# Another order for the hand-written list of steps of slots 0 to 6 in an RWKV-7 and squared-ReLU kernel

## The chip, the cores and the metric

The kernel runs on one core of a Trainium2 chip. The metric is the device time of one execution in microseconds (us): the median of three runs for the kernel before, and a profiled execution beside it.

## What is computed

Two blocks follow each other. The first is a linear recurrence with a state of 40 x 40 for each of 4 batches and 8 heads, over 768 steps:

```python
for t in range(S):
    y[:, :, t] = np.einsum('bhd,bhde->bhe', rt, state)
    Sa = np.einsum('bhde,bhe->bhd', state, at)
    state = state * wt[:, :, None, :] - np.einsum('bhd,bhe->bhde', Sa, bt) + np.einsum('bhd,bhe->bhde', vt, kt)
```

The second takes y as 3072 tokens of 320 numbers: `h = max(x @ w_in, 0)`, then `out = (h * h) @ w_out`, with a hidden width of 2048. The weights come in 64-bit floats, which the kernel turns into 32-bit floats itself.

## The kernel before

The 768 steps are cut into 6 chunks of 128, and a slot is one chunk of one batch with all its 8 heads: 24 slots, numbered with the batches inside the chunk, so that slots 0 to 3 are the first chunk of the four batches and start from an empty state. In a slot the recurrence becomes matrix products. What remains serial in it is the inverse of a triangular matrix for each head, which is made in small blocks by POOL (GpSimd), for one or more slots at a time; such a group is a unit. Unit 0 is slot 0, unit 1 slot 1, unit 2 slots 2 and 3, unit 3 slots 4 and 5, unit 4 slots 6 and 7, and so on.

A slot passes through these steps. Each has a short word in the list that this change is about; the digit behind the word is the slot (for S, K the unit; for W, pa, pd a piece of the weights; for f a width).

- LW, LA, lk, lb, lr, lv: fetches of w, of b and a, and of k, b, r, v, each 160 KB from device memory into a ring of tiles. A fetch waits until the tile's last reader is done.
- e1.1 to e1.6, "early" (line 361): PE turns w, DVE (VectorE) makes running products of it (lines 372 to 381), PE turns b and a, DVE scales them (387, 388), PE multiplies them, and ACT (ScalarE) copies the product N out of PSUM (398 to 402). N is a single buffer.
- sE, sN: N's blocks are stored to device memory for POOL (kept_q, line 420), and the decays (kept_e, line 390). D loads decays back into one of two tiles.
- K (take, line 440): POOL's load of a unit's N blocks. S (solving, line 458): POOL's row-by-row solve; S3.99 runs it to its end and issues the store of the answer (kept_t, line 482).
- B (line 508): the load of the answer, A: of N. J, four times (lines 515 to 534): the inverse put together, DVE and ACT first, then two small sets of products on PE with ACT copies between.
- k, a, kb, rv, mrv: products of k, r, v with the decays, masked by DVE (line 347).
- x, then c seven times: the chain of the slot. Its fourth c is a set of transposes, its sixth the masked product RX, and its last gives the tokens (line 692) and the new state. ds and ts scale and turn the state where there is one.
- mv: eight DMAs that gather two slots' tokens for the second block. th and wh make the hidden layer for a quarter of it, sq squares it on DVE, q does a part of the second product.
- W: fetch of a piece of the weights. pa and pd: the ACT and the DVE instructions of one step that turns a piece into 32-bit floats (lines 275 to 292). pa copies one piece and finishes the one before; pd needs pa's result, and the next pa needs pd's.
- f: fill-in matmuls (line 264), identity times identity, whose result nobody reads. f10 makes ten blocks of 128 columns in matmuls of at most four blocks.

The slots from 7 on run through a function with a fixed order. Slots 0 to 6, with the early steps of up to slot 13, are issued by one list of 484 words, in which each word issues its instructions at once:

```python
        word, _, queue = word.partition("@")
        on_queue[0] = {"": nc.sync, "a": nc.scalar, "g": nc.gpsimd}[queue]
```

Each engine takes its instructions in the list's order, and each DMA is issued by the SP (SyncE) queue, or by ACT's or POOL's where the word ends in @a or @g. Nothing else schedules: a semaphore wait holds everything behind it on its engine. Weights have to be ready in 27 steps (pd26) before the first q. Two PSUM pools matter: ps_w with four banks, in which a transposed or multiplied tile stays until DVE or ACT has read it, and ps_f with two for the second block and the fill-ins.

Of the kernel before, what the change touches and what calls it, by code (L numbers as in the profile page):

```python
# [17 lines left out]
def kernel(  # L18
# [82 lines left out]
    def tick():  # L101
        for entry in line:
            entry[0] -= 1
        while line and line[0][0] <= 0:
            line.pop(0)[1]()
# [766 lines left out]
    def advance(u, n_):  # L872
        if u not in solves:
            solves[u] = [-1, solving(u, range(100))]
        while solves[u][0] < n_ and next(solves[u][1], "end") != "end":
            solves[u][0] += 1
        if n_ > 90:
            run(solves[u][1])
# [46 lines left out]
    }  # L925

    for word in """
e0.1 lv0 e0.2 e0.3 e0.4 e0.5 e0.6 sN0 K0 e1.1 e1.2 e1.3 e1.4 e1.5 f3 LW2 LA2 e1.6 sN1 LW3 S0.12 K1 k0 a0 rv0 mrv0 e2.1 kb0 f6 e2.2 lk1 LA3 LW4 lv1 e2.3 e2.4 e3.1 x0 e3.2 e2.5 sE2 f10 e2.6 sN2 e3.3 e3.4 e3.5 f8 sE3 f6 e3.6 LA4 f44 lv2 lr1 LW5 S0.99 B0 J0 S1.8 S1.20 sN3 K2 W0@g S1.99 J0 J0 f6 W1 rv1 lr2 f2 mrv1 c0 e4.1 e4.2 e4.3 k1 W2@g LA5 B1 c0 c0 kb1 e4.4 e4.5 sE4 c0 c0 c0 pa0 c0 D2 LW6 lb2 a1 e4.6 lk2 pd0 pa1 f10 pd1 J1 x1 f4 pa2 pd2 W3 sN4 A2 pa3 pd3 rv2 f4 e5.1 e5.2 J1 f24 lv3 J1 f3 c1 LA6 mrv2 f6 c1 lr3 e5.3 S2.4 S2.99 c1 f6 e5.4 c1 e5.5 sE5 B2 k2 f6 c1 kb2 a2 c1 c1 mv0 pa4 pd4 W4 pa5 pd5 e5.6 sN5 J2 K3 lk3 A3 lb3 D3 S3.99 LA7 e6.1 e6.2 f30 f10 x2 e6.3 e6.4 e6.5 f4 J2 rv3 J2 c2 c2 f4 c2 pa6 pd6 e6.6 f14 c2 mrv3 k3 pa7 B3 LW7 J3 c2 c2 kb3 lr4 sE6 J3 lv4 e7.1 pd7 c2 a3 f1 f4 pa8 J3 lk4@a e7.2 W5 x3 lv5 lb4 A4 D4 sN6 f8 rv4 W8 B4 W6 W7 c3 c3 e7.3 pd8 pa9 pd9 pa10 ds4 mrv4 e7.4 LA8 LW8 e7.5 c3 J4 k4 sE7 pd10 W11 f4 f8 c3 e7.6 W10 lr5 J4 sN7 c3 K4 pa11 pd11 kb4 J4 pa12 pd12 c3 W12 ts4 pa13 W9 f4 a4 pd13 W13 c3 pa14 D5 B5 mv1 pd14 e8.1 e8.2 LA9 f4 x4 W14 lb5 A5 lk5 pa15 pd15 pa16 f2 pd16 ds5 c4 rv5 f12 pa17 pd17 pa18 pd18 W15@a f2 th0 J5 pa19 pd19 W16 mrv5 c4 wh0 pa20 pd20 pa21 lr6 th0 c4 pd21 e8.3 lv6 LW9 wh0 W17 pa22 c4 e8.4 e8.5 LA10 k5 c4 kb5 c4 e8.6 pd22 W18@a sN8 th0 sE8@a wh0 J5 ts5 LW10 a5 th0 wh0 sq0 c4 D6 W19 sq0 e9.1 pa23 A6 lk6 S4.99 J5 e9.2 e9.3 x5 lb6 B6 e9.4 c5 f2 e9.5 sE9@a pd23 W20 e9.6 sN9 LW11 K5 rv6 lv7 LA11 pa24 ds6 e10.1 LW12 c5 e10.2 pd24 pa25 pd25 mrv6 e10.3 k6 J6 pa26 pd26 c5 th0 wh0 e10.4 LA12 e10.5 sE10@g lr7 c5 c5 th0 J6 kb6 c5 e10.6 sN10 e11.1 LW13 c5 a6 ts6 lk7 e11.2 sq0 mv2 wh0 x6 J6 D7 e11.3 e11.4 q0 e11.5 sq0 e11.6 sN11@g S5.99 K6 S6.99 q0 e12.1 q0 q0 e12.2 e12.3 c6 sE11 rv7 lb7 A7 c6 B7 q0 mrv7 q0 wh0 q0 e12.4 q0 ds7 J7 e12.5 c6 k7 kb7 th0 sq0 J7 a7 c6 sE12 e12.6 lr8 c6 LW14 ts7 wh0 c6 th0 th0 LA13 wh0 sN12 e13.1 e13.2 LA14 c6 q0 e13.3 e13.4 e13.5 x7 J7 A8 lv8 B8 e13.6 q0 lb8 sN13 D8 lk8 sq0 sE13 K7 S7.99
""".split():
        word, _, queue = word.partition("@")  # L930
        on_queue[0] = {"": nc.sync, "a": nc.scalar, "g": nc.gpsimd}[queue]
        kind = word.rstrip("0123456789.")
        at = word[len(kind):]
        if kind == "S":
            advance(*(int(n_) for n_ in at.split(".")))
        else:
            kinds[kind](int(at.split(".")[0]))
        on_queue[0] = nc.sync
        tick()
# [85 lines left out]
    for i in range(LAID, len(order)):  # L1025
        tc.no_sync_barrier()
        g = ready.pop(i)
# [41 lines left out]
```

## Time and profile before

| what | value |
|---|---|
| runs | 952.27, 954.84, 956.72 us; median 954.84 |
| profiled execution | 959.58 us, of which 957.7 us are the span from the first to the last instruction |
| PE (TensorE) busy | 913.9 us, 95% of the span |
| DVE, ACT, POOL busy | 451.0, 287.4, 531.9 us |
| mean granted PE clock | 0.959 of full speed |
| PE busy, list's part (0 to 337.7 us) | 299.4 us, of it fill-ins 73.6 us |
| DMA packets | 253222, of them 234143 under 512 bytes |

An fp32 matmul shows as two rows on PE and a transpose as one. A row's duration depends on the granted clock. A wait is put down to the semaphore that came last, so an engine that had long been done is not its cause.

### The profile page before, as it was taken

How to read it: one execution, taken by the hardware profiler on the slowest of the kernel's cores; microseconds unless marked ns; L12 is line 12 of the kernel's file. 1: busy time of each engine (PE TensorE's matmuls, PEld its weight loads, DVE VectorE, ACT ScalarE, POOL GpSimd, SP SyncE). 2: the span in 40 equal slices, each digit the busy share in tenths (PEclk: the TensorE clock that was granted, in tenths of full speed). 3: DMA queues.
4: the chain of work that ended last, by engine and by line, in shares of the span. 5: the costliest groups of instructions: out<-in, count | busy, mean ns of one | idle time of the engine just before them, and what ended most of it. 6: DMA issues, size and time to landing. Idle time of an engine off the chain costs nothing.

```text
span 957.7 us, 22644 instructions
## 1 busy us (share of the span) xinstructions
PE 913.9 (95%) x9156; PEld 725.4 (76%) x9156; DVE 451.0 (47%) x1064; ACT 287.4 (30%) x735; POOL 531.9 (56%) x1001
## 2 busy tenths in 40 slices
PE   5989989798999999999999999999999999999998
PEld 4646656567787887878888888888888887887776
DVE  4517556797873454543655553643334332231111
ACT  3123234545432333332433332222212222222111
POOL 4788507347007686429999849999858860000000
PEclk8888788889899999999999999999999999999999
DMA  9689757767784677895564786505474254120000
GB/s 110 116 158 186 145 117 140 162 167 152 151 134 115 130 153 133 165 178 109 113 96 91 122 177 116 110 21 84 105 138 76 38 108 76 40 36 9 13 14 14
DMA packets 253222, 103.36 MB, mean 108 GB/s; under 512 B 234143, under 2 KB 240159, under 8 KB 251967
## 3 DMA queue, kind: packets, MB, share of 16 engines
q1 hardware_dynamic: 246869, 83.43, 48.5%
q0 software_dynamic: 3600, 16.25, 6.8%
q10 hardware_dynamic: 2650, 2.25, 0.9%
q8 instruction: 72, 1.18, 0.5%
q14 instruction: 31, 0.25, 0.1%
HBM read 69.00 MB, written 30.92 MB: 104 GB/s over the span
## 4 chain that ended last, share of the span: by engine, by line
PE 72%; DMA 4%; DVE 2%; ACT 2%; SPq 1%; issue 0%; ACTq 0%; DVEq 0%
PE ps_f L87 40%; PE ps_w L87 13%; PE ps_c L87 12%; PE ps_w L331 4%; DMA dec<-kept_e 2%; DMA spares<-kept_m 2%; PE ps_c L593 1%; PE ps_c L666 1%; PE ps_w L577 1%; DMA hid<-in_moe_w_out_dram 1%; ACT N L401 0%; SPq L508 0%; DMA kept_t<-half_t 0%; SPq L146 0%; SPq L110 0%
## 5 line engine op out<-in xcount | busy, mean ns | idle before, releaser
L477 POOL TENSOR_TENSOR half_p<-half_n,half_t 128x126 f32<-128x126 f32 (+44 forms) x437 | 232.6, 532 | 75.7 <-DMA half_n<-kept_q 19.8
L479 POOL TENSOR_TENSOR half_t<-half_t,half_p 128x126 f32<-128x126 f32 (+44 forms) x437 | 249.1, 570 | 34.3
L87 PE MATMUL ps_f<-w_out,hid 128*128 128x320 f32 x768 | 218.7, 436 | 0.0
L87 PEld LDWEIGHTS ps_f<-w_out,hid 128*128 128x128 f32 x768 | 142.0, 190 | 54.0 <-issue 0.2
L87 PE MATMUL ps_f<-tokens,w_in 128*128 128x256 f32 x672 | 159.2, 391 | 0.0
L87 PEld LDWEIGHTS ps_f<-tokens,w_in 128*128 128x128 f32 x672 | 127.6, 195 | 19.5 <-issue 2.0
L764 DVE TENSOR_TENSOR hid<-hid 128x512 f32<-128x512 f32 x96 | 81.1, 883 | 50.1 <-ACT hid L757 49.7
L757 ACT ACTIVATE hid<-ps_f 128x512 f32<-128x512 f32 x84 | 50.0, 597 | 83.5 <-PE ps_f L87 83.5
L264 PE MATMUL ps_f<-ident 128*128 128x512 f32 (+2 forms) x148 | 73.6, 637 | 0.0
L347 DVE TENSOR_TENSOR RV<-ps_w,upper 128x512 f32<-128x512 f32 x48 | 30.9, 686 | 51.1 <-PE ps_w L87 50.8
L451 POOL DMA_DIRECT2D half_n<-kept_q x18 | 9.5, 530 | 80.1 <-DMA kept_q<-N 53.5
L692 DVE TENSOR_TENSOR tokens<-ps_c,dec 128x512 f32<-128x512 f32 x24 | 16.6, 690 | 76.6 <-PE ps_c L87 76.6
L372 DVE TENSOR_TENSOR_SCAN decay<-ps_w,ones 128x64 f32<-128x64 f32 x88 | 23.8, 271 | 59.7 <-PE ps_w L331 59.6
L264 PEld LDWEIGHTS ps_f<-ident 128*128 128x128 f32 x148 | 30.4, 223 | 27.5 <-issue 26.6
L347 DVE TENSOR_TENSOR RX<-ps_w,upper 128x512 f32<-128x512 f32 x48 | 30.9, 686 | 41.4 <-PE ps_w L87 41.0
L87 PE MATMUL ps_f<-tokens,w_third 64*128 64x256 f32 x336 | 46.9, 392 | 3.1 <-ACT hid L757 3.1
L543 DVE TENSOR_TENSOR kvT<-ps_w,dec 128x512 f32<-128x512 f32 x24 | 16.5, 688 | 63.1 <-ACT minus_x L653 36.0
L87 PEld LDWEIGHTS ps_c<-xr,T 64*64 64x64 f32 x768 | 28.5, 141 | 19.6 <-issue 16.5
L398 ACT COPY N<-ps_w 128x256 f32<-128x256 f32 x48 | 17.7, 368 | 83.8 <-PE ps_w L87 47.4
L555 ACT COPY rT<-ps_w 128x512 f32<-128x512 f32 x24 | 14.0, 585 | 77.7 <-PE ps_w L331 77.6
L87 PEld LDWEIGHTS ps_f<-tokens,w_third 64*128 64x128 f32 x336 | 31.0, 192 | 6.5 <-ACT hid L757 3.7
L87 PE MATMUL ps_c<-xr,T 64*64 64x40 f32 x768 | 34.5, 235 | 1.4 <-ACT xr L660 0.8
(146 smaller groups left out, 1407.3 us busy)
## 6 DMA issues: line engine op xcount, KB each, us to landing
dec<-kept_e SPq DMA_DIRECT2D x22, 633.8 KB
kept_e<-decay SPq DMA_DIRECT2D x19, 633.8 KB
in_w<-in_w_dram SPq DMA_DIRECT2D x24, 160.0 KB
in_b<-in_b_dram SPq DMA_DIRECT2D x24, 160.0 KB
in_ab<-in_a_dram SPq DMA_DIRECT2D x24, 160.0 KB
in_r<-in_r_dram SPq DMA_DIRECT2D x24, 160.0 KB
in_v<-in_v_dram SPq DMA_DIRECT2D x24, 160.0 KB
out_dram<-o SPq DMA_DIRECT2D x24, 160.0 KB
```

Source lines behind the costliest of these rows:

```text
L87: nc.tensor.matmul(o, l_, r_, start=start, stop=True, skip_group_check=True)
L264: nc.tensor.matmul(fill_bank[:, :n * 128], ident, ident.unsqueeze(1).to_broadcast([128, n, 128]), start=True, stop=True, skip_group_check= ...
L331: nc.tensor.transpose(p_[:, q * 128:(q + 1) * 128], pair(x_, q), ident)
L347: nc.vector.tensor_tensor(t_, p_, over4(upper), Alu.mult)
L372: nc.vector.tensor_tensor_scan(up[:, q, MID + 1:C + 1], wT[:, q, MID:], ones, 1.0, Alu.mult, Alu.mult)
L398: nc.scalar.copy(plain, p_[:, ::2].rearrange("s h (f t) -> s f h t", f=2))
L477: nc.gpsimd.tensor_tensor(p_, part[:, at:at + m_].unsqueeze(1).to_broadcast([128, n, m_]), t3[:, :n, s:s + 1].to_broadcast([128, n, m_]), ...
L479: nc.gpsimd.tensor_tensor(t3[:, :n, s + 1:], t3[:, :n, s + 1:], p_, Alu.subtract)
L543: nc.vector.tensor_tensor(kT, kT_, down[:, :, 1:C + 1], Alu.mult)
L692: nc.vector.tensor_tensor(t_, y_, g["up"][:, :, :C], Alu.mult)
L757: nc.scalar.activation(h_, p_.rearrange("p f t -> p (f t)"), Act.Relu)
L764: nc.vector.tensor_tensor(h_, h_, h_, Alu.mult)
```

## The change

The list of words is replaced by another order of the same words. Three kinds of things differ: places of words, one queue (lk7 goes from SP to ACT), and the fill-ins. Four f4 go, and one each of f6, f8, f10 and f12 come: 281 blocks for 261, 80 matmuls for 74. Slots 7 to 23 are not touched. The list has one line; here it is broken at the changed places, and unchanged stretches between are left out.

```diff
-... f3 LW2 LA2 e1.6 sN1 LW3 ... kb0 f6 e2.2 lk1 LA3 LW4 lv1 e2.3
+... f3 LW2 e1.6 sN1 LA2 LW3 ... kb0 f6 lk1 LA3 LW4 lv1 e2.2 e2.3
...
-sE2 f10 e2.6 sN2 e3.3 e3.4 e3.5 f8 sE3 f6 e3.6 LA4 f44
+sE2 f10 f8 e2.6 sN2 e3.3 e3.4 e3.5 e3.6 sE3 f6 LA4 f44
...
-B1 c0 c0 kb1 e4.4 e4.5 sE4 c0 c0 c0 pa0 c0 D2 LW6 lb2 a1 e4.6 lk2 pd0 pa1 f10 pd1 J1 x1 f4 pa2 pd2 W3 sN4
+B1 c0 c0 c0 kb1 e4.4 e4.5 sE4 c0 c0 pa0 c0 lk2 pd0 D2 LW6 lb2 a1 e4.6 pa1 f10 pd1 J1 x1 f12 pa2 pd2 W3 lv3 sN4
...
-e5.2 J1 f24 lv3 J1 f3 c1 LA6 mrv2 f6 c1 lr3 e5.3 S2.4 S2.99 c1 f6 e5.4 c1 e5.5
+e5.2 J1 f24 J1 f3 c1 LA6 e5.3 mrv2 S2.4 S2.99 f6 c1 lr3 c1 f6 c1 e5.4 e5.5
-sE5 B2 k2 f6 c1 kb2 a2 c1 c1 mv0 pa4 pd4 W4 pa5 pd5 e5.6 sN5
+sE5 B2 k2 f6 c1 c1 c1 kb2 a2 mv0 f8 pa4 pd4 W4 pa5 pd5 e5.6 sN5
-J2 K3 lk3 A3 lb3 D3 S3.99 LA7 e6.1 e6.2 f30 f10 x2 e6.3 e6.4 e6.5 f4 J2
+e6.1 e6.2 f30 x2 e6.3 e6.4 J2 K3 lk3 A3 lb3 S3.99 LA7 D3 f10 e6.5 J2
...
-pd7 c2 a3 f1 f4 pa8 J3 lk4@a e7.2 W5 x3 lv5 lb4 A4 D4 sN6 f8 rv4 W8 B4 W6 W7 c3 c3
+pd7 pa8 c2 a3 f10 f1 J3 lk4@a e7.2 W5 x3 lv5 lb4 A4 f8 rv4 W8 D4 sN6 f6 W6 W7 B4 c3 c3
-e7.3 pd8 pa9 pd9 pa10 ds4 mrv4 e7.4 LA8 LW8 e7.5 c3 J4 k4 sE7 pd10 W11 f4 f8 c3 e7.6
+e7.3 pd8 pa9 pd9 pa10 mrv4 e7.4 e7.5 LA8 LW8 c3 J4 k4 sE7 pd10 W11 f8 c3 e7.6
-W10 lr5 J4 sN7 c3 K4 pa11 pd11 kb4 J4 pa12 ... W13 c3 pa14 D5 ... W14 lb5 A5
+W10 lr5 sN7 c3 K4 pa11 J4 pd11 ds4 kb4 J4 pa12 ... W13 pa14 c3 D5 ... W14 A5
...
-c4 pd21 e8.3 lv6 LW9 wh0 W17 pa22 c4 e8.4 e8.5 LA10 k5 c4 kb5 c4 e8.6 pd22 W18@a sN8
+c4 wh0 W17 pd21 lv6 c4 e8.3 e8.4 e8.5 LA10 LW9 k5 c4 c4 kb5 e8.6 pa22 pd22 W18@a W19 sN8
-wh0 J5 ts5 LW10 a5 th0 wh0 sq0 c4 D6 W19 sq0 e9.1 pa23 A6 lk6 S4.99 J5 e9.2 e9.3
+wh0 ts5 LW10 a5 J5 th0 wh0 sq0 c4 D6 e9.1 pa23 A6 lk6 S4.99 J5 e9.2 sq0 e9.3
...
-ts6 lk7 e11.2 sq0 mv2 wh0 x6 J6 D7 e11.3 e11.4 q0 e11.5 sq0 e11.6 sN11@g S5.99 K6 S6.99 q0 e12.1 q0 q0 e12.2 e12.3
+ts6 lk7@a e11.2 sq0 mv2 wh0 D7 e11.3 e11.4 x6 J6 q0 e11.5 q0 e11.6 sN11@g S5.99 K6 S6.99 e12.1 q0 q0 e12.2 sq0 e12.3
-c6 sE11 rv7 lb7 A7 c6 B7 q0 mrv7 q0 wh0 q0 e12.4
+c6 lb7 sE11 rv7 B7 A7 wh0 q0 c6 q0 q0 mrv7 e12.4
-e12.5 c6 k7 kb7 th0 sq0 J7 a7 c6 sE12 e12.6 lr8 c6 LW14 ts7 wh0 c6 th0 th0 LA13 wh0 sN12 e13.1
+e12.5 sE12 c6 k7 kb7 th0 a7 sq0 J7 c6 c6 c6 e12.6 ts7 wh0 th0 th0 LA13 lr8 LW14 e13.1 wh0 sN12
-c6 q0 e13.3 e13.4 e13.5 x7 J7 A8 lv8 B8 e13.6 q0 lb8 sN13 D8 lk8 sq0 sE13 K7 S7.99
+c6 e13.3 e13.4 x7 J7 q0 A8 lv8 B8 e13.5 e13.6 q0 lb8 sN13 sq0 D8 sE13 K7 lk8 S7.99
```

In the line with W14, lb5 stands behind W16 in the new order. Of the smaller moves e10.2 passes LW12.

More of the change, by code (lines that the diff above doesn't have):

```diff
@@ L927 @@
     for word in """
-e0.1 lv0 e0.2 e0.3 e0.4 e0.5 e0.6 sN0 K0 e1.1 e1.2 e1.3 e1.4 e1.5 f3 LW2 LA2 e1.6 sN1 LW3 S0.12 K1 k0 a0 rv0 mrv0 e2.1 kb0 f6 e2.2 lk1 LA3 LW4 lv1 e2.3 e2.4 e3.1 x0 e3.2 e2.5 sE2 f10 e2.6 sN2 e3.3 e3.4 e3.5 f8 sE3 f6 e3.6 LA4 f44 lv2 lr1 LW5 S0.99 B0 J0 S1.8 S1.20 sN3 K2 W0@g S1.99 J0 J0 f6 W1 rv1 lr2 f2 mrv1 c0 e4.1 e4.2 e4.3 k1 W2@g LA5 B1 c0 c0 kb1 e4.4 e4.5 sE4 c0 c0 c0 pa0 c0 D2 LW6 lb2 a1 e4.6 lk2 pd0 pa1 f10 pd1 J1 x1 f4 pa2 pd2 W3 sN4 A2 pa3 pd3 rv2 f4 e5.1 e5.2 J1 f24 lv3 J1 f3 c1 LA6 mrv2 f6 c1 lr3 e5.3 S2.4 S2.99 c1 f6 e5.4 c1 e5.5 sE5 B2 k2 f6 c1 kb2 a2 c1 c1 mv0 pa4 pd4 W4 pa5 pd5 e5.6 sN5 J2 K3 lk3 A3 lb3 D3 S3.99 LA7 e6.1 e6.2 f30 f10 x2 e6.3 e6.4 e6.5 f4 J2 rv3 J2 c2 c2 f4 c2 pa6 pd6 e6.6 f14 c2 mrv3 k3 pa7 B3 LW7 J3 c2 c2 kb3 lr4 sE6 J3 lv4 e7.1 pd7 c2 a3 f1 f4 pa8 J3 lk4@a e7.2 W5 x3 lv5 lb4 A4 D4 sN6 f8 rv4 W8 B4 W6 W7 c3 c3 e7.3 pd8 pa9 pd9 pa10 ds4 mrv4 e7.4 LA8 LW8 e7.5 c3 J4 k4 sE7 pd10 W11 f4 f8 c3 e7.6 W10 lr5 J4 sN7 c3 K4 pa11 pd11 kb4 J4 pa12 pd12 c3 W12 ts4 pa13 W9 f4 a4 pd13 W13 c3 pa14 D5 B5 mv1 pd14 e8.1 e8.2 LA9 f4 x4 W14 lb5 A5 lk5 pa15 pd15 pa16 f2 pd16 ds5 c4 rv5 f12 pa17 pd17 pa18 pd18 W15@a f2 th0 J5 pa19 pd19 W16 mrv5 c4 wh0 pa20 pd20 pa21 lr6 th0 c4 pd21 e8.3 lv6 LW9 wh0 W17 pa22 c4 e8.4 e8.5 LA10 k5 c4 kb5 c4 e8.6 pd22 W18@a sN8 th0 sE8@a wh0 J5 ts5 LW10 a5 th0 wh0 sq0 c4 D6 W19 sq0 e9.1 pa23 A6 lk6 S4.99 J5 e9.2 e9.3 x5 lb6 B6 e9.4 c5 f2 e9.5 sE9@a pd23 W20 e9.6 sN9 LW11 K5 rv6 lv7 LA11 pa24 ds6 e10.1 LW12 c5 e10.2 pd24 pa25 pd25 mrv6 e10.3 k6 J6 pa26 pd26 c5 th0 wh0 e10.4 LA12 e10.5 sE10@g lr7 c5 c5 th0 J6 kb6 c5 e10.6 sN10 e11.1 LW13 c5 a6 ts6 lk7 e11.2 sq0 mv2 wh0 x6 J6 D7 e11.3 e11.4 q0 e11.5 sq0 e11.6 sN11@g S5.99 K6 S6.99 q0 e12.1 q0 q0 e12.2 e12.3 c6 sE11 rv7 lb7 A7 c6 B7 q0 mrv7 q0 wh0 q0 e12.4 q0 ds7 J7 e12.5 c6 k7 kb7 th0 sq0 J7 a7 c6 sE12 e12.6 lr8 c6 LW14 ts7 wh0 c6 th0 th0 LA13 wh0 sN12 e13.1 e13.2 LA14 c6 q0 e13.3 e13.4 e13.5 x7 J7 A8 lv8 B8 e13.6 q0 lb8 sN13 D8 lk8 sq0 sE13 K7 S7.99
@@ new lines @@
+e0.1 lv0 e0.2 e0.3 e0.4 e0.5 e0.6 sN0 K0 e1.1 e1.2 e1.3 e1.4 e1.5 f3 LW2 e1.6 sN1 LA2 LW3 S0.12 K1 k0 a0 rv0 mrv0 e2.1 kb0 f6 lk1 LA3 LW4 lv1 e2.2 e2.3 e2.4 e3.1 x0 e3.2 e2.5 sE2 f10 f8 e2.6 sN2 e3.3 e3.4 e3.5 e3.6 sE3 f6 LA4 f44 lv2 lr1 LW5 S0.99 B0 J0 S1.8 S1.20 sN3 K2 W0@g S1.99 J0 J0 f6 W1 rv1 lr2 f2 mrv1 c0 e4.1 e4.2 e4.3 k1 W2@g LA5 B1 c0 c0 c0 kb1 e4.4 e4.5 sE4 c0 c0 pa0 c0 lk2 pd0 D2 LW6 lb2 a1 e4.6 pa1 f10 pd1 J1 x1 f12 pa2 pd2 W3 lv3 sN4 A2 pa3 pd3 rv2 f4 e5.1 e5.2 J1 f24 J1 f3 c1 LA6 e5.3 mrv2 S2.4 S2.99 f6 c1 lr3 c1 f6 c1 e5.4 e5.5 sE5 B2 k2 f6 c1 c1 c1 kb2 a2 mv0 f8 pa4 pd4 W4 pa5 pd5 e5.6 sN5 e6.1 e6.2 f30 x2 e6.3 e6.4 J2 K3 lk3 A3 lb3 S3.99 LA7 D3 f10 e6.5 J2 rv3 J2 c2 c2 f4 c2 pa6 pd6 e6.6 f14 c2 mrv3 k3 pa7 B3 LW7 J3 c2 c2 kb3 lr4 sE6 J3 lv4 e7.1 pd7 pa8 c2 a3 f10 f1 J3 lk4@a e7.2 W5 x3 lv5 lb4 A4 f8 rv4 W8 D4 sN6 f6 W6 W7 B4 c3 c3 e7.3 pd8 pa9 pd9 pa10 mrv4 e7.4 e7.5 LA8 LW8 c3 J4 k4 sE7 pd10 W11 f8 c3 e7.6 W10 lr5 sN7 c3 K4 pa11 J4 pd11 ds4 kb4 J4 pa12 pd12 c3 W12 ts4 pa13 W9 f4 a4 pd13 W13 pa14 c3 D5 B5 mv1 pd14 e8.1 e8.2 LA9 f4 x4 W14 A5 lk5 pa15 pd15 pa16 f2 pd16 ds5 c4 rv5 f12 pa17 pd17 pa18 pd18 W15@a f2 th0 J5 pa19 pd19 W16 lb5 mrv5 c4 wh0 pa20 pd20 pa21 lr6 th0 c4 wh0 W17 pd21 lv6 c4 e8.3 e8.4 e8.5 LA10 LW9 k5 c4 c4 kb5 e8.6 pa22 pd22 W18@a W19 sN8 th0 sE8@a wh0 ts5 LW10 a5 J5 th0 wh0 sq0 c4 D6 e9.1 pa23 A6 lk6 S4.99 J5 e9.2 sq0 e9.3 x5 lb6 B6 e9.4 c5 f2 e9.5 sE9@a pd23 W20 e9.6 sN9 LW11 K5 rv6 lv7 LA11 pa24 ds6 e10.1 e10.2 LW12 c5 pd24 pa25 pd25 mrv6 e10.3 k6 J6 pa26 pd26 c5 th0 wh0 e10.4 LA12 e10.5 sE10@g lr7 c5 c5 th0 J6 kb6 c5 e10.6 sN10 e11.1 LW13 c5 a6 ts6 lk7@a e11.2 sq0 mv2 wh0 D7 e11.3 e11.4 x6 J6 q0 e11.5 q0 e11.6 sN11@g S5.99 K6 S6.99 e12.1 q0 q0 e12.2 sq0 e12.3 c6 lb7 sE11 rv7 B7 A7 wh0 q0 c6 q0 q0 mrv7 e12.4 q0 ds7 J7 e12.5 sE12 c6 k7 kb7 th0 a7 sq0 J7 c6 c6 c6 e12.6 ts7 wh0 th0 th0 LA13 lr8 LW14 e13.1 wh0 sN12 e13.2 LA14 c6 e13.3 e13.4 x7 J7 q0 A8 lv8 B8 e13.5 e13.6 q0 lb8 sN13 sq0 D8 sE13 K7 lk8 S7.99
```

## The prediction

> **What bounds the kernel now.** I read four views in order: engine busy time on either side of the end of the list, the chain of work that ended last, the waits of each engine in the list's part, and the timeline around the places where the new order differs. The last matmul of the list ends at 337.7 us (found by counting matmuls in list order), so I asked for busy time in two stretches.
>
> ```profile
> 0.00:337.70 337.70, 299.44 (x2993) 223.12 (x2994) 203.05 (x541) 122.55 (x321) 178.55 (x486) 0.89 0.73 141
> 337.70:957.70 620.00, 614.50 (x6165) 502.24 (x6163) 247.99 (x523) 164.84 (x415) 353.38 (x516) 1.00 0.48 90
> ```
>
> The columns are PE, PEld, DVE, ACT and POOL busy (instructions), then granted clock, DMA share and GB/s. Behind the list PE is busy 614.5 of 620 us at full clock: that part issues the same instructions in both kernels, so I hold it at 620. In the list's part PE is idle 337.7 - 299.4 = 38.3 us, and 73.6 us of its busy time are fill-in matmuls (line 264, 148 rows), which compute nothing. The change can only work on these 112 us and on matmuls that ran at half clock.
>
> The chain of work says where the list's part is held up:
>
> ```profile
> 177.53 2.34 DMA kept_t<-half_t
> ...
> 198.88 9.37 DMA dec<-kept_e
> ...
> 212.57 3.75 DMA hid<-in_moe_w_out_dram
> ...
> 217.99 1.61 PE ps_f L87 x8
> ```
>
> From 218 us it is nearly all matmuls; ahead of that it hangs on POOL's solve (kept_t is the answer of unit 3), then on the decays of slot 5. The timeline shows what these wait for:
>
> ```profile
> 91.79 5.42 PE L264 MATMUL ps_f<-ident 128*128 128x512 f32 x12
> 98.11 1.08 PE L87 MATMUL ps_w<-blocks,spares 32*32 32x32 f32 x32 [0.90 <-ACT spares L527]
> ...
> 120.17 6.56 SPq L705 DMA_DIRECT2D tokens<-tokens  x8
> 126.83 3.35 SPq L257 DMA_DIRECT2D w_out<-in_moe_w_in_dram  x4
> 130.29 0.94 SPq L420 DMA_DIRECT2D kept_q<-N  x2
> ...
> 138.34 1.05 POOL L451 DMA_DIRECT2D half_n<-kept_q  x2 [26.97 <-DMA kept_q<-N]
> ...
> 183.00 0.45 DVE L515 STREAM_TRANSPOSE spares<-blocks 128x256 f32<-128x256 f32 x1 [3.65 <-DMA blocks<-kept_t]
> ...
> 188.66 0.49 DVE L284 SCALAR_TENSOR_TENSOR hid<-hid 128x320 int32<-128x320 int32 x1 [2.17 <-ACT hid L275]
> ```
>
> POOL sits 27 us until slot 5's N has been stored (kept_q). That store stands on SP's queue behind the move of group 0's tokens and fetch W4. POOL then solves unit 3 until 177.5; SP passes the answer on (B4), and DVE has waited 3.65 us when it lands. So the line is: tokens of slot 1, SP's queue, K3, S3, B4, J4, the rounding on DVE, D5, the FFN.
>
> **What the Trainium skill says.** "TensorE: Matmul & The Clock Gate", What's actually happening: PE has two clocks, half and full; about 3.4 us of activity gives the full one, an idle window takes it away, and the window runs free of the kernel, so the moment differs from run to run. The trace agrees: the granted clock alternates between 0.50 and 1.00 in stretches of 3.4 to 13.7 us, and a fill-in row takes 0.43 to 0.45 us at full clock (22 rows in 9.71 us at 45.9) but 0.81 at 178.5 (6 rows in 4.86). "DMA: Bandwidth & Descriptors", Issuing engines are not separate DMA queues: all issuing engines share 16 DMA engines and another issuer saves only its issue time. The trace agrees: D5, issued at 198.9 in 0.34 us, needs 9.37 us to land. The same page, Specifications, asks for 512 bytes a packet; here 108929 of 118128 packets ahead of 337.7 us are smaller, and DMA share is 0.73.
>
> **The change, part by part.** POOL's program is the same; SP has 264 for 265 instructions, ACT 330 for 329, because lk7 goes from SP to ACT; DVE has the same ones in another order. PE gets 80 for 74 fill-in matmuls, 160 for 148 rows.
>
> *Ahead of 68 us.* LA2 goes behind sN1 on SP: two 160 KB fetches (20.4 to about 25.7 us at the end of their issue) that e2.4 reads at 33.3; some 7 us are left. It also leaves K0's load alone, worth -1 to 0 us of POOL, but J1 is held by DVE's pd1 until 90.6 anyway: nothing. If the fetch were late, e2.4 to e2.6 would slip with it. f8 goes ahead of e2.6: 4 rows of 0.43 are 1.7 us in a gap of 0.9, so slot 2's N is 0.8 us late. That delays slot 3's N (ACT, 48.6) too, and both have until K2 at 64.4: nothing. If SP's queue carried it to B0, c0 would be 0.8 later, and POOL's unit 1 would hide that at J1.
>
> *68 to 111 us.* lk2, lv3 and D-loads change places on SP; their readers (k2 at 112, mrv3 behind rv3 at 135) leave over 15 us. pd0 ahead of a1 on DVE moves 1.8 us of rounding before 1.3 us of A; x1 follows at 86.4 either way, since A would end at 86.0. f4 becomes f12: 4 more rows, 1.74 us. PE has 0.41 us of idle time ahead of J1's first products and 0.90 ahead of its second ones, which wait for ACT behind the rounding step pa3: 1.74 - 0.41 - 0.90 = +0.4 us for c1. If the rows ran at half clock, 4 x 0.81 - 0.9 = +2.3. Behind mrv2 the transposes of c1 pass e5.4, and e5.3 passes mrv2 on DVE: their order on PE costs nothing, 0.6 us earlier for c1's ACT copy.
>
> *111 to 138 us, the main gain.* The last two steps of c1 go ahead of kb2 and a2. On PE, RX's products start behind f6 at 114.1 instead of at 115.6; on DVE they no longer stand behind kb2 (0.9) and A (1.29). Token row 119.45 becomes about 117.5: -1.9. What goes behind it, kb2 and a2, ends DVE at 121.5 for 121.1, so pd4 is 0.4 later, pa5 and slot 5's N (ACT, 127.6) become 128.0. SP starts the token move 1.9 earlier, ends W4 at 128.3, and can store N at 128.4 for 130.3. Net of the +0.4 above: K3 is 1.5 us earlier. The f8 behind it and the six words from e6.1 to e6.4 ahead of J2 stand in PE's and DVE's wait for J2 (30 + 10 and 4 fill-in columns become 8 + 30 + 10): nothing.
>
> *158 to 200 us.* POOL is continuous in S3, so B4's answer lands 1.5 us earlier. In SP's queue W6 and W7 no longer wait behind B4 (181.3, for about 172); pa11, which reads W6, ran at 188.0, so that is hidden. f10 for f4 ahead of J3, and f6 ahead of c3, cost up to 1.0 us each, in front of rv4 and of ACT's 176.1 to 177.2 rounding: hidden. On DVE ds4 (0.85) leaves the front of RV; f4 (2 rows, 1.6 us cold) leaves the front of c3. So c3 and e7.6 are ready for J4 at about 181.5. pa11 now goes ahead of J4's copies on ACT; it saves 0.75 of the 2.17 us that DVE waited, and ds4 takes 0.85 back. I keep 0.5 of these: c3's tokens, and so D5 and slot 5, are 1.5 + 0.5 = 2.0 us earlier.
>
> *200 us to the end.* The rounding on DVE and D5's landing (208.3, DVE waits 0.17) move together: -2.0 at 218. RX ahead of kb5 meets the PSUM rows that bT still holds (0.23 us wait at 228.96): +0.3. W19, x6 with J6, q0, sq0, A7, B7, lr8 and e13.5 move inside stretches where PE never idles (264.7 to 337.7 busy throughout) and their data is not due for some us; free; late data would show there as PE idle time, one for one. lk7 costs ACT an issue of some 0.5 us (0.48 for lk4 at 164.87) ahead of e11.2, where ACT waited 2.82 us. One q0 ahead of e11.6 delays POOL's S5 by 2.4 us; its answer, ready at 324, is asked for at 334.4.
>
> *The clock.* Cut at its steps, the busy-time view shows ten half-clock stretches in the list's part, 75 us together, 48 of them behind 90 us. The new rows stand in or ahead of three of them (from 100.9, 175.9 and 138.4), and a wait less makes one less likely. I count one window of 3.4 us less on PE-bound work: 1.7 us. Bounds: 0 gain or 3.4 us lost (one 6.8 us stretch more), and 4.9 us gained, half of the 9.76 us that PE was busy from 100.9 to 111.1.
>
> Sum: -2.0 + 0.3 - 1.7 = -3.4 us. The profiled execution took 959.58 us (span 957.7 and 1.9 around it), so 956.2; it stood 4.7 above the median of the three runs, 954.84. From the median: 951.4.
>
> **Rivals.** *A larger gain, 947 us:* the stretch from 100.9 to 111.1 runs at full clock. PE is bound there, c1 is 4.9 us earlier, K3 and J4 follow until DVE's 3.65 us wait is used up, -2.0 + 0.3 - 1.7 as above and at most another 3.65 + 0.9 from DVE's two waits: -3.4 - 4.5 = about -8. For it: the fill-ins now reach 98.7 without a hole. Against: the window is free-running. *Nothing, 955 us:* D5's 9.37 us is the engines' load, not its issue; at 213.5 to 220.3 the DMA share is full, so an earlier issue lands no earlier and 218 stays. Against it: 0.42 of DMA share from 210.1 to 213.5. *Slower, 960 us:* f12's four rows stay at half clock. That is +2.3 at J1, and c1 behind it runs cold for a further 6.8 us, 3.4. At +1.9 the token gain is gone; at 5.7 K3 and J4 are 3.8 later, and with one window more instead of less, 1.7, the sum is 3.8 - 0.5 + 0.3 + 1.7 = +5.3. For it: the stretch at 100.9 began behind just such fill-ins. That the order isn't what runs is excluded: each engine takes its instructions in the program's order.
>
> **How the numbers follow.** The stated case 0.34 (own range 949 to 953.5, a bit over a third of it below the half per cent line), larger gain 0.28, nothing 0.22, slower 0.16. Half a per cent, 4.8 us, is about what a measurement of this kernel can tell from no change: faster is under 950.07, slower over 959.6. Faster: 0.13 + 0.28 = 0.41; slower: 0.14 of the last case; same: 0.45. The range from 945 to 960 leaves out a third of the larger gain's (0.09) and somewhat over half of the slow case (0.09).
>
> **What would show it.** Right: token row of slot 1 about 2 us earlier, POOL's wait for kept_q ending near 137, the transpose of J4 near 181.5, D5 near 197, list end near 334, and 620 us behind it. Wrong: POOL's wait ends at 138 or later; J1's second step is later than 99; half-clock stretches after 90 us exceed the 48 us of before; or the part behind the list differs from 620 by over 2 us, which no step here allows.

## The result, and the profile after

The changed kernel takes 961.90 us, median of 20 runs (956.62 to 967.71), beside 957.17 us for the kernel before (20 runs, 952.27 to 960.61): ratio 1.0061, 95% interval 1.0045 to 1.0078. So it is about 5 us slower, where 951.4 was forecast. The profiled execution doesn't show that: 959.45 us (span 957.5), against 959.58 for the profile before. Its mean granted clock, 0.976, is the highest of the 20 runs (median 0.966); that of the profile before was 0.959. So two things have to be explained: where the forecast gain went, and why this pair of profiles doesn't show the loss.

Busy time of the changed kernel on both sides of the end of its list (the columns are those of the prediction's first view):

```profile
0.00:333.40 333.40, 293.64 (x3004) 218.56 (x3005) 202.89 (x541) 121.03 (x321) 176.80 (x484) 0.94 0.75 143
333.40:957.50 624.10, 615.56 (x6165) 503.50 (x6163) 248.68 (x523) 164.62 (x415) 352.25 (x518) 0.99 0.47 89
```

The list ends at 333.4 us for 337.7, 4.3 us earlier, as forecast (334). But the part behind it, which issues the same instructions, takes 624.1 us for 620.0, so nothing is left at the end. In the list's part of the changed kernel the chain of work that ended last has these transfers and this first large group of matmuls:

```profile
177.35 2.29 DMA blocks<-kept_t
...
199.73 1.83 DMA tokens<-tokens
...
215.71 2.55 PE ps_f L87 x7
```

The stretch that is nearly all matmuls starts at 215.7 where it started at 218.0. D5's landing has left the chain. The timeline at the places that the prediction showed:

```profile
99.80 1.07 PE L87 MATMUL ps_w<-blocks,spares 32*32 32x32 f32 x32 [1.59 <-ACT spares L527]
...
115.12 0.69 DVE L692 TENSOR_TENSOR tokens<-ps_c,dec 128x512 f32<-128x512 f32 x1 [1.18 <-PE ps_c L87]
119.18 6.30 SPq L705 DMA_DIRECT2D tokens<-tokens  x8
...
137.37 1.04 POOL L451 DMA_DIRECT2D half_n<-kept_q  x2 [23.77 <-DMA kept_q<-N]
...
179.73 0.45 DVE L515 STREAM_TRANSPOSE spares<-blocks 128x256 f32<-128x256 f32 x1 [4.75 <-DMA blocks<-kept_t]
183.85 0.49 DVE L284 SCALAR_TENSOR_TENSOR hid<-hid 128x320 int32<-128x320 int32 x1 [0.64 <-ACT hid L275]
```

The tokens of slot 1 are 4.3 us earlier (119.45 to 115.12), their move only 1.0, since SP is late itself, and POOL starts unit 3 at 137.4 for 138.3. In this profile PE ran at full clock from 97 to 117 us, where the mean before was 0.74.

Now slot 9, the one slot behind the list that differs (PE begins it at 411.9 before and 407.7 after, and slot 10 at 448.9 and 448.8). The timeline of the kernel before:

```profile
413.21 2.74 SPq L110 DMA_DIRECT2D kept_d<-N  x4
418.12 1.04 POOL L451 DMA_DIRECT2D half_n<-kept_d  x2 [22.33 <-DMA kept_n<-N]
418.69 1.25 SPq L493 DMA_DIRECT2D spares<-kept_m  x2
429.13 0.96 PE L87 MATMUL ps_w<-spares 32*32 32x32 f32 x32 [0.70 <-DMA spares<-kept_m]
430.02 1.16 PE L87 MATMUL ps_w<-rT,xnT 40*128 40x128 f32 x16
```

and of the changed kernel:

```profile
408.96 4.24 SPq L110 DMA_DIRECT2D kept_d<-N  x4
415.17 1.03 POOL L451 DMA_DIRECT2D half_n<-kept_d  x2 [23.25 <-DMA kept_d<-N]
415.93 1.43 SPq L493 DMA_DIRECT2D spares<-kept_m  x2
428.03 1.26 PE L87 MATMUL ps_w<-spares 32*32 32x32 f32 x32 [3.85 <-DMA spares<-kept_m]
429.22 2.08 PE L87 MATMUL ps_w<-rT,xnT 40*128 40x128 f32 x16
```

In slot 9 SP stores the N of slot 17 (kept_d, for POOL), then loads slot 10's answer, its N and kept_m, the blocks of N that PE's 32 x 32 products need. POOL's load of unit 8, 768 KB, starts within 1 us of kept_m. PE needs kept_m some 16.5 us into the slot. Before, it was issued 6.8 us into the slot and landed just in time; now it is issued 8.2 us in. SP begins the stores ahead of it 1.3 us into the slot in both kernels, but takes 4.24 us to issue them, for 2.74. From kept_m's issue to PE's start it is 12.1 us for 10.4; PE waits 3.85 us, and then falls to half clock: the matmuls behind take 2.08 and 1.92 us for 1.16 and 1.07. The sum: wait +3.15, the three groups at half clock +0.30 + 0.92 + 0.85, less 1.07 for a half-clock stretch of before that fell on two later groups: +4.15, and the slot takes 41.1 us for 37.0.

### The profile page after: what moved, and what is told of

The parts are those of the page before. It is cut to its first block, busy times and chain, and to the rows that moved or that the text cites. A ratio compares the mean times of both kernels' runs of the same rounds, so it can differ in the third digit from the quotient of the medians.

```text
span 957.5 us, 22669 instructions
## 1 busy us (share of the span) xinstructions
PE 909.2 (95%) x9168; PEld 722.0 (75%) x9168; DVE 451.6 (47%) x1064; ACT 285.6 (30%) x735; POOL 529.0 (55%) x1001
## 4 chain that ended last, share of the span: by engine, by line
PE 81%; DVE 5%; DMA 4%; POOL 4%; ACT 3%; issue 2%; SPq 1%; ACTq 0%; POOLq 0%; DVEq 0%
PE ps_f L87 40%; PE ps_w L87 16%; PE ps_c L87 13%; PE ps_w L331 5%; PE ps_f L264 3%; DMA w_out<-in_moe_w_in_dram 2%; POOL half_t L479 1%; POOL half_p L477 1%; PE ps_c L666 1%; PE ps_c L593 1%; DMA spares<-kept_m 1%; PE ps_w L577 1%; SPq L508 1%; DMA kept_e<-decay 1%; ACT N L401 0%
## 5 line engine op out<-in xcount | busy, mean ns | idle before, releaser
L87 PE MATMUL ps_f<-tokens,w_in 128*128 128x256 f32 x672 | 155.9, 385 | 0.0
L87 PEld LDWEIGHTS ps_f<-tokens,w_in 128*128 128x128 f32 x672 | 125.4, 192 | 17.9 <-issue 1.3
L347 DVE TENSOR_TENSOR RX<-ps_w,upper 128x512 f32<-128x512 f32 x48 | 30.9, 686 | 40.5 <-PE ps_w L87 40.1
L543 DVE TENSOR_TENSOR kvT<-ps_w,dec 128x512 f32<-128x512 f32 x24 | 16.5, 687 | 59.6 <-ACT minus_x L653 34.9
L565 DVE TENSOR_TENSOR f<-end,dec 128x4 f32<-128x4 f32 x20 | 7.2, 361 | 66.4 <-DMA dec<-kept_e 66.4
```

What stands on the lines that cost most here:

```text
L87: nc.tensor.matmul(o, l_, r_, start=start, stop=True, skip_group_check=True)
L347: nc.vector.tensor_tensor(t_, p_, over4(upper), Alu.mult)
L543: nc.vector.tensor_tensor(kT, kT_, down[:, :, 1:C + 1], Alu.mult)
```

## The experiments

A ratio is to the kernel before on the same chip. Every kernel also left a profile, so that the list's end (PE's begin of slot 7), slot 9 and the clock can be compared in 20 profiles.

**One part of the new order alone.** The list was cut at places where both orders have issued the same words but for fill-ins: LA4, the second J2, pa14. Each kernel takes the new order in one of four stretches and the old one elsewhere; its diff is the lines of the change's diff in that stretch.

```diff
 part1: the lines from "LW2" to "LA4"             (LA2, f8)
 part2: the lines from "B1 c0 c0" to "f10 e6.5 J2" (f12, tokens of slot 1, J2)
 part3: the lines from "pd7" to "W13"             (B4, J4, pa11, ds4)
 part4: the lines from "W14" to the end           (the tail)
```

> The new order up to LA4 (the first 52 words), the old one behind it. The sum's theory (the first stretch is hidden): 0, within 1 us of before. Rival, the head pays: the f8 ahead of e2.6, which the trace of the changed kernel shows as 1.9 us on e2.6, 2.0 on slot 2's store and on the first c0, isn't taken back later: 2 to 5 us slower. Rival, the loss sits behind the list: about 0 as well, since the list's end would not move.

> The old order up to LA4 and from the second J2 on, the new one between (f12, the token rows of slot 1 ahead of kb2 and a2). The sum's theory: list end 2 us earlier and the time 1 to 2 us shorter. Rival, the wait in slot 9 (kept_m, 3.85 us in the changed kernel's profile for 0.70) takes any gain: list end 1 to 3 us earlier, slot 10 begins where it did, time within 1 us of before. Rival, the part behind the list was made worse by how the tail of the list is ordered: then this part alone keeps its gain to the end.

> The new order between the second J2 and pa14 alone (B4, J4, pa11, ds4, W6 and W7, the fill-ins there). The sum's theory: without an earlier B4 only the rounding steps gain, 0 to 1 us. Rival, the wait in slot 9: within 1 us of before whatever the list's end does. Rival, the loss is in this part: 2 to 5 us slower with a later D5.

> The new order from c3 in front of D5 on alone (W19, the J5, J6, J7 and q0 moves, lk7 on ACT, LW14, lr8, lk8 later). The sum's theory: +0.3 from RX ahead of kb5, so 0 to 1 us slower. Rival, the tail pays: the later fetches, q0 ahead of S5 and the DMAs of lk7 and lk8 make slots 7 to 10 wait for transfers: 3 to 6 us slower, with PE idle behind 338 us beyond the 5.5 us of before. Rival, the wait in slot 9 only gives back what the list gains: within 1 us of before, since nothing is gained here.

| kernel | ratio (95% interval) | list ends, us | slot 9, us |
|---|---|---|---|
| part1 | 1.0020 (0.9997 to 1.0043) | 335.8 | 36.3 |
| part2 | 0.9988 (0.9968 to 1.0007) | 332.4 | 39.5 |
| part3 | 1.0005 (0.9986 to 1.0023) | 335.9 | 39.8 |
| part4 | 1.0023 (1.0004 to 1.0042) | 338.6 | 40.1 |

Part1 is called the head below, part2 the middle, part4 the tail. No part carries the loss alone. The middle has the sign of the forecast, the head and the tail the other one, and the tail's is the only interval clear of 1. The ratios' excesses add up to 0.36% of the 0.61%. In part2 and part3 slot 9 takes 39.5 and 39.8 us although the tail is the old one; the table of slot 9 below comes back to them.

**Second profiles of both kernels.**

> The kernel before once more, for a second profile. If slot 9's wait for kept_m is where the difference lies, PE's stay in slot 9 (411.9 to 448.9, 37.0 us in the first profile, about 34.5 without a wait) is 37 to 40 us again and the rest behind 338 us is as it was to 0.5 us. If it lies elsewhere behind the list, another slot differs by over 1 us from the first profile.

> The changed kernel once more, for a second profile. If its list is really 4 us shorter, slot 7 begins at 332 to 335 us again and slot 9 again takes 40 to 42 us. If the first profile was a lucky list (half-clock stretches 44 us against 75), slot 7 begins at 336 to 340 and the list is no better than that of before.

Before: 959.84 us, list end 337.3, slot 9 37.3. After: 958.58 us, list end 332.9, slot 9 40.5. The other slots agree to 0.3 us. So slot 9 is where the part behind the list differs, each time: 40.8 us for 37.1 in the mean of the two. That is 3.7 of the 4.7 us of the result; the remaining one is not assigned.

**Slot 10's loads moved out of slot 9.** One line, in both kernels; the blocks, N and kept_m of slot 10 then stand in slot 8 of the program, ahead of slot 17's store:

```diff
-    soon = lambda i: i < 2 * B or unit_of[i - 1] == unit_of[i]
+    soon = lambda i: i < 2 * B or unit_of[i - 1] == unit_of[i] or i == 10
```

> The kernel before with the loads of slot 10's answer, N and kept_m issued in slot 8 instead of in slot 9, ahead of the store of slot 17's N and so ahead of POOL's load of unit 8 (768 KB), with which they compete. Nothing else differs on any engine. Theory of the wait in slot 9: the 0.7 to 2 us wait and the half clock behind it go, slot 9 takes about 34.6 us, 1.5 to 3 us faster. Rival, the loss lies elsewhere (list or another slot): within 1 us of before.

> The changed kernel with the same early loads for slot 10. Theory of the wait in slot 9: the 3.85 us wait and its half clock go, 5 to 7 us less than the changed kernel, and the list's 2 to 4 us show: faster than the old order with the same loads by 2 to 4 us. Rival, the new list itself is slower in most runs: it stays 2 to 5 us slower than the old order with the same loads.

The old order with it: 954.15 us, 0.9949 (0.9926 to 0.9971). The new order with it: 956.82 us, 0.9985 (0.9963 to 1.0006). In both, slot 9 takes 34.3 us and PE doesn't wait in it. SP's and PE's rows in the old order with the loads, where slot 9 begins at 412.9:

```profile
413.00 1.45 SPq L508 DMA_DIRECT2D blocks<-kept_t  x2
...
415.17 2.51 SPq L493 DMA_DIRECT2D spares<-kept_m  x2
...
418.39 4.66 SPq L110 DMA_DIRECT2D kept_d<-N  x4
...
429.31 0.69 PE L87 MATMUL ps_w<-spares 32*32 32x32 f32 x32
```

SP issues them no sooner than 0.1 us into PE's slot 9, so in time they move by less than a slot: kept_m is issued 2.3 us into the slot for 6.8 (in the new order 5.5 for 8.2). They are now ahead of slot 17's stores and of POOL's load, which waits for these. The new order with the early loads is 0.76% better than the changed kernel, 7 us, about what slot 9 is shorter (34.3 us for 41.1). The wait and the half clock behind it cost the old order something too. The rival isn't beaten, though: the new list stays behind the old one.

And the list in the profile of the new order with early loads, the same instructions as in the changed kernel, ended at 339.9 us, 6.5 later than in the first profile. Part of this begins between 97 and 117 us. Busy time there, first in the changed kernel's profile (the last three columns are granted clock, DMA share and GB/s):

```profile
97.00:117.00 20.00, 17.68 (x221) 12.73 (x221) 13.09 (x35) 7.36 (x18) 13.80 (x34) 1.00 0.90 157
```

and in that of the same list with the early loads:

```profile
97.00:117.00 20.00, 18.19 (x129) 12.18 (x127) 10.28 (x28) 7.08 (x18) 12.59 (x31) 0.66 0.87 150
```

221 matmul rows against 129 in the same 20 us. At POOL's load of unit 3 the lag is 2.3 us (139.7 for 137.4), at D5's issue 5.2 (202.1 for 196.9), so this stretch is not the whole of the 6.5. Over all 20 profiles, by the clock in this window and the order between LA4 and the second J2:

| clock, 97 to 117 us | list end, old order there | list end, new order there |
|---|---|---|
| 1.00 | 332.9, 334.3 | 332.2, 332.4, 332.8, 333.4, 333.8 |
| 0.74 to 0.83 | 335.8, 335.9, 337.3, 337.7, 338.6 | 332.9, 333.7, 333.9, 335.5 |
| 0.66 | 337.9, 338.6 | 335.2, 339.9 |

The list's end moves with the half-clock stretch that begins near 100 us, in either order: by means, 333.6 us without it and 337.4 with it in the old order, 332.9 and 335.2 in the new. This is a correlation over 20 profiles and no experiment, and in the new order one profile (339.9) makes much of the difference. Still, a pair of profiles can't measure 2 us in the list.

**Which word makes kept_m late.** First the q0 ahead of e11.6, put back in the new order and moved alone in the old one:

```diff
 after_q:  -q0 e11.5 q0 e11.6 sN11@g S5.99 K6 S6.99 e12.1
           +q0 e11.5 e11.6 sN11@g S5.99 K6 S6.99 q0 e12.1
 before_q: -sq0 e11.6 sN11@g S5.99 K6 S6.99 q0 e12.1
           +sq0 q0 e11.6 sN11@g S5.99 K6 S6.99 e12.1
```

> The changed kernel with one word back in its old place: the second q0 stands behind S6.99 again instead of ahead of e11.6; on the engines only eight matmuls of PE change places. Theory of POOL's lateness: unit 5's solve starts 46.8 us ahead of slot 7 as in the kernel before instead of 45.2, unit 7's load comes 1 us sooner, kept_m is issued 7 to 7.5 us into slot 9 for 7.8 to 8.2, its wait there is 1 to 2 us for 2.8 to 3.9, 1 to 3 us faster than the changed kernel. Rival, SP's own order (kept_e of slot 13 ahead of k of slot 8) makes SP late: the wait stays at 2.8 us or more and the time where it is.

> The kernel before with that one word moved as in the change: one q0 ahead of e11.6. Theory of POOL's lateness: kept_m issued 7.8 to 8.4 us into slot 9 for 6.8, a wait of 2 to 3.5 us for 0.7 to 1.2, 1 to 3 us slower. Rival, SP's own order: kept_m at 6.8 to 7.4, within 1 us of before.

The old order with the q0 moved: 1.0021 (1.0002 to 1.0041), kept_m issued 8.4 us into slot 9, and

```profile
428.19 0.87 PE L87 MATMUL ps_w<-spares 32*32 32x32 f32 x32 [3.16 <-DMA spares<-kept_m]
429.00 1.88 PE L87 MATMUL ps_w<-rT,xnT 40*128 40x128 f32 x16
```

In this profile one word is enough for the wait and the half clock. The new order with it put back: 959.55 us, 1.0018 (0.9998 to 1.0038), 0.43% better than the changed kernel; but its profile still has kept_m at 8.4 us, a wait of 3.70 us and a slot 9 of 41.0, so the expected 1 to 2 us wait is a miss, and where the 0.43% lie is not shown. Then the other candidate, lk8 behind sE13:

```diff
 after_q_lk8 (on top of after_q): -sq0 D8 sE13 K7 lk8 S7.99
                                  +D8 lk8 sq0 sE13 K7 S7.99
 before_lk8:                      -D8 lk8 sq0 sE13 K7 S7.99
                                  +D8 sq0 sE13 K7 lk8 S7.99
```

> The changed kernel with the second q0 behind S6.99 and, at the list's end, lk8 back ahead of sq0 and sE13 as in the kernel before. If both together make SP late: kept_m issued 6.8 to 7.4 us into slot 9, a wait of 0.7 to 1.8 us, as fast as the kernel with q0 put back alone or 1 to 2 us faster. If neither does in the new list: a wait of 2.5 us or more, within 1 us of the kernel with q0 put back alone.

> The kernel before with lk8 behind sE13 and K7 as in the change; only this load of SP's changes its place. If SP's order makes kept_m late: issued 7.8 us or more into slot 9, a wait of 2 to 3 us for 0.7 to 1.2, 1 to 3 us slower. If not: kept_m at 6.8 to 7.4, within 1 us of before.

With both words in their old places the new order takes 955.33 us, 0.9983 (0.9954 to 1.0012): 0.78% better than the changed kernel, with no overlap of the intervals, and level with the kernel before. Over the q0 alone it is 0.35% better, with overlap. Its slot 9:

```profile
411.12 2.76 SPq L110 DMA_DIRECT2D kept_d<-N  x4
...
416.60 1.50 SPq L493 DMA_DIRECT2D spares<-kept_m  x2
...
426.92 0.91 PE L87 MATMUL ps_w<-spares 32*32 32x32 f32 x32 [0.57 <-DMA spares<-kept_m]
427.76 1.16 PE L87 MATMUL ps_w<-rT,xnT 40*128 40x128 f32 x16
```

The stores take 2.76 us to issue again, kept_m goes out 6.7 us into the slot, and the slot takes 35.1 us, 6.0 less than in the changed kernel; 0.78% are 7.5 us. In the old order lk8 alone gave a wait of 2.67 us in its profile (kept_m at 8.0 us), but 0.9994 (0.9970 to 1.0018) in time: that it costs anything alone is not shown. All profiles without the early loads:

| q0 and lk8 | kept_m issued, us into slot 9 | PE's wait, us | slot 9, us |
|---|---|---|---|
| both old: before (two), part1, part2, part3, after_q_lk8 | 6.8, 6.8, 7.4, 7.4, 8.0, 6.7 | 0.70, 1.17, 1.74, 1.73, 2.21, 0.57 | 37.0, 37.3, 36.3, 39.5, 39.8, 35.1 |
| q0 new: before_q | 8.4 | 3.16 | 40.9 |
| lk8 new: before_lk8, after_q | 8.0, 8.4 | 2.67, 3.70 | 40.5, 41.0 |
| both new: part4, after (two), after_head | 8.4, 8.2, 7.8, 9.2 | 2.90, 3.85, 2.75, 3.99 | 40.1, 41.1, 40.5, 42.7 |

The waits don't overlap, though narrowly: 2.21 us at most with both old, 2.67 at least with one new. The times of kept_m's issue do (8.0 in part3, 7.8 in the second profile of the changed kernel). Means of slot 9: 37.5 and 41.0 us; part2 and part3 had the half clock with both words old.

A rival is that a list that ends earlier meets the same transfer later in the slot: the six profiles with both old end their lists at 335.8 us in the mean, the seven others at 334.1. It can't be the whole: part4 ends its list at 338.6 and waits 2.90 us, part2 ends its at 332.4 and waits 1.73.

**The head put back.**

```diff
-LW2 e1.6 sN1 LA2 ... lv1 e2.2 e2.3 ... f10 f8 e2.6 sN2 e3.3 e3.4 e3.5 e3.6 sE3 f6 LA4
+LW2 LA2 e1.6 sN1 ... f6 e2.2 lk1 ... e2.3 ... f10 e2.6 sN2 e3.3 e3.4 e3.5 f8 sE3 f6 e3.6 LA4
```

> The changed kernel with the old order up to LA4 (no f8 ahead of e2.6). If the head costs what ten profiles show of it (the first c0 begins 49.9 us behind e1.6's start for 48.6) and this reaches the end: 1 to 3 us faster than the changed kernel, 0.3 to 0.5% slower than before. Rival, c0 to K3 swallows it: as slow as the changed kernel, 0.5 to 0.7%.

1.0033 (1.0016 to 1.0049): 0.28% under the changed kernel, the size that part1 gave from the other side (0.20%). Neither difference is sure: the interval of part1 reaches below 1, and this one overlaps that of the changed kernel. This profile has the longest slot 9 of all.

**What the list is worth without slot 9's wait.** All with the early loads: the middle alone; the old tail; the old head and the old stretch from J2 to pa14; the new list with q0 and lk8 put back; and beside the last the old list again.

```diff
 mid_load10:          part2 and the early loads
 oldtail_load10:      part1, part2, part3 and the early loads
 newtail_load10:      part2, part4 and the early loads
 after_q_lk8_load10:  after_q_lk8 and the early loads
 before_load10_again: before_load10
```

> The old order with the new one only between LA4 and the second J2 (the token rows of slot 1 ahead of kb2 and a2, f12), and slot 10's loads issued in slot 8. If the middle alone is worth its 1 to 3 us: 0.6 to 0.8% faster than before, 1 to 3 us under the old order with the same loads (0.51%). If the gain of the middle was chance: 0.4 to 0.55%, the same as the old order with the loads.

> The new order up to pa14, the old one from c3 ahead of D5 on, and slot 10's loads in slot 8. If the head and the stretch from J4 to D5 cause what is left (0.36%): as slow against before as the new list with the same loads, 0.1 to 0.25% faster. If the tail causes it: as the old list with the same loads or better, 0.5 to 0.7% faster.

> The old order up to LA4 and between the second J2 and pa14, the new one in the other two stretches (tokens of slot 1, and the tail), and slot 10's loads in slot 8. If the head and the stretch from J4 to D5 cause what is left: 0.5 to 0.7% faster than before. If the tail causes it, in slot 10 or in the list: 0.1 to 0.3% faster.

> The changed kernel with the second q0 and lk8 in their old places and slot 10's loads in slot 8. If the new list is worth the predicted 3.4 us: 0.8 to 0.95% faster than before, that is 0.3 to 0.4% faster than the old list with the same loads. If it is worth nothing over many runs, and the 4 us of the two profiles were half-clock stretches that happened to fall elsewhere: 0.4 to 0.6% faster than before, the same as the old list with the loads.

> The old list with slot 10's loads in slot 8 once more, beside the run above: 0.4 to 0.6% faster than before, slot 9 at 34.3 us, no wait for kept_m in it.

| kernel, all with early loads | ratio (95% interval) |
|---|---|
| old list (first series) | 0.9949 (0.9926 to 0.9971) |
| mid_load10 | 0.9946 (0.9927 to 0.9965) |
| oldtail_load10 | 0.9958 (0.9938 to 0.9978) |
| newtail_load10 | 0.9957 (0.9938 to 0.9976) |
| after_q_lk8_load10 | 0.9969 (0.9951 to 0.9988) |
| old list (beside it) | 0.9971 (0.9951 to 0.9991) |

On one chip the new list, with q0 and lk8 in their old places, and the old one are equal, 954.29 and 953.92 us, though the spans of their profiles lay 5.6 us apart in favour of the new one (list ends 332.2 and 337.9). So the 3.4 us forecast for the list aren't there: the two intervals leave room for a list better or worse by some 2.6 us. The middle alone, for which 0.6 to 0.8% was expected if its gain is real, stands at 0.54%, where the old list stands at 0.51 and 0.29%: its gain doesn't show in the timed runs. That the whole new list with early loads stood at 0.9985, and neither its tail nor the rest of it reproduced that, stays open. Its profile shows POOL's load of unit 8 2.7 us later into slot 9 than in the old list (14.8 for 12.1) and slot 10 at 35.6 us for 34.3, which would fit the same lateness of SP one slot on.

The kernels of this table beat both the kernel before and the changed one; the simplest is the old list with the one changed line.

The 20 profiles also show three stretches inside the list that the prediction priced. Their means by the order in them (runs with the old and with the new one):

| stretch | old order, us | new order, us | difference | forecast |
|---|---|---|---|---|
| begin of e1.6 to begin of the first c0 on PE | 48.7 (12) | 49.7 (8) | +1.0 | 0 |
| that c0 to POOL's K3 | 70.0 (9) | 68.7 (11) | -1.3 | -1.5 |
| B4 to D5, by SP's issues | 19.1 (11) | 20.3 (9) | +1.2 | -0.5 |

In the profiles the middle gains what it should, and the other two give it back. The stretches between and behind these are shorter in the new order by 1.1 us each (K3 to B4, by the middle's order, and D5 to the list's end, by the tail's), so that all five make -1.3 us. Profiles with more or less half clock are mixed in these means; the timed runs above show no gain of the list.

## Why the prediction was wrong

*The part behind the list.* It was held at 620 us because the instructions are the same. Same instructions aren't the same time: slot 9 took 4.1 us more in the first profile, and 3.5 us more in the means of the profiles with and without the two words q0 and lk8 in new places. The prediction named this as a thing that no step allowed, and it happened.

*The step that failed* is the last clause on the stretch from 200 us: "One q0 ahead of e11.6 delays POOL's S5 by 2.4 us; its answer, ready at 324, is asked for at 334.4." The delay was seen (1.6 us against the begin of slot 7), and its answer was indeed in time. What was not followed is what POOL does next: unit 6, then the load of unit 7, which starts 23.8 us into slot 7 for 22.8, beside SP's fetches. In the kernel before, where slot 7 begins at 337.7:

```profile
360.49 1.04 POOL L451 DMA_DIRECT2D half_n<-kept_q  x2
```

and in the changed kernel, where it begins at 333.4:

```profile
357.24 1.03 POOL L451 DMA_DIRECT2D half_n<-kept_q  x2
```

Two slots later SP begins slot 17's stores at the same point of the slot, but takes 1.5 us longer to issue them, so kept_m goes out 1.4 us later and PE waits 3.85 us for 0.70. "The Trainium skill" was cited for what such transfers do to each other: all issuing engines share 16 DMA engines ("DMA: Bandwidth & Descriptors", Issuing engines are not separate DMA queues). The prediction applied this to D5 and not to POOL's loads; that the sharing is what makes the stores' issue longer, no run here shows. The move of lk8 behind sE13 wasn't priced at all. That the two words together cost what the changed kernel lost is shown by the kernel that puts both back (0.78%, wait 0.57 us for 3.85). The path between is argued: why the stores take longer to issue, and how 1 us at unit 7's load leads there, was not followed transfer by transfer.

*Ahead of 68 us* f8 was put at 0.8 us and hidden. e2.6's end in the first profile is 1.9 us later, and SP did carry it on to B0 (its issue ends at 58.7 for 57.0), the case that the prediction had set aside; c0 starts 1.0 us later in the mean. This also set off a sign of being wrong: J1's second step begins at 99.8 us, later than 99, and counted from c0 it is no later than before (29.6 us for 29.9). What reaches the end, 0.2 to 0.3%, is within the intervals.

*68 to 138 us* was right in mechanism and size in the profiles: tokens earlier, SP's move and store behind them, 1.3 us at K3 in the mean for a forecast of 1.5. The 4.3 us of the token row in the first profile, for a forecast of 1.9, are in part the clock's (1.00 for 0.74 from 97 to 117 us).

*158 to 200 us.* J4's transpose came at 179.7 for a forecast of 181.5. The 0.5 us for pa11 and ds4 had the wrong sign: from B4 to D5 the old order takes 18.2 to 19.6 us and the new one 19.9 to 20.6, without overlap. In the first profiles three things differ there: pa11 now stands in front of J4's copies on ACT, which begin 7.6 us after B4 for 7.4, although PE is ready 1.3 us sooner; the next step of c3 met half clock (2.1 us for 1.3); and ds4 stands on DVE between pd11 and kb4. Which of them makes the 1.2 us was not tested.

*The clock* was counted as one window less, 1.7 us. In the first profile of the changed kernel half-clock stretches behind 90 us in the list make 27 us, for 48 before, far more than one window; in its list with early loads the stretch near 100 us was back. The bounds were of the right size, 4.9 gained and 3.4 lost, but not their weight: in profiles with the stretch near 100 us the list ends 2.3 to 3.8 us later by means, as much as all moves together were to bring, and 13 of the 20 profiles have it. The rivals "larger gain" and "slower" were this mechanism from its two sides, and one and the same list ended at 333.4 us without the stretch and at 339.9 with it. But neither is why the median is 961.9: the rivals looked for the loss at J1, and most of it was in slot 9. The rival "slower" named 960 us; that the measured time lies near it is chance.

*The base.* From 951.4 to 961.9 are 10.5 us: 3.4 of gain that isn't there, 4.7 of loss, and 2.3 because the kernel before has a median of 957.17 in 20 runs, where three gave 954.84. The forecast was made on one profiled execution. The first two of the old list ended at 337.7 and 337.3, and those of the new one at 333.4 and 332.9, which looked like the forecast come true; many executions show no such difference.

## What to carry to other kernels

A delay that its own consumer can absorb must be followed to the next transfer of the same engine: what it moves there may meet a transfer with no slack. Where a load has to land just as it is needed, and a large load of another queue starts beside it, it was worth more here to issue it ahead of the stores in front of it (0.3 to 0.5%, one line) than to reorder the work before it. A gain smaller than what one half-clock stretch moves is measured over many executions, never in a pair of profiles.

## What the runs showed of the hardware

The Trainium skill, "TensorE: Matmul & The Clock Gate" (Why this matters for your kernels) advises no PE idle gaps over about 3 us. Here half clock came with shorter ones too: in slot 9 waits of 1.73, 2.21 and 2.67 us went with 6.8 us at half clock, while those of 0.57 and 1.74 us went with none and those of 0.70 and 1.17 us with 3.4 us. All eight profiles with 2.2 us or more show a half-clock stretch of at least 6.8 us there. Shortly ahead of the wait stand transposes (20 rows in 2.4 us), right behind it small matmuls, 32 x 32; whether these matter too, the runs don't tell.
